# First loads in one ordered queue, with the other queue held, in a fused linear-attention and expert-mixture kernel

## The chip, the cores and the metric

The kernel runs on one core of one Trainium2 chip. A core has a matrix engine (TensorE, "PE" in the profile; "PEld" are its weight loads), a vector engine (VectorE, "DVE"), an activation engine (ScalarE, "ACT"), a general engine (GpSimd, "POOL") and a queue engine (SyncE, "SP") that issues transfers. ACT and POOL can issue transfers too. The metric is the device time of one execution in microseconds; the smaller the better.

## The reference

Inputs are q, k and v, each of 8 batches, 8 heads, 576 rows and 64 columns in float32, and the weights of a mixture of 4 experts (512 to 1024 to 512) with a table of 4608 x 4 expert shares.

```python
phi = lambda x: where(x > 0, x, exp(x) - 1) + 1
kv  = einsum('bhsd,bhse->bhde', phi(k), v);  z = sum(phi(k), axis=2)
x   = einsum('bhsd,bhde->bhse', phi(q), kv) / (einsum('bhsd,bhd->bhs', phi(q), z)[..., None] + 1e-6)
x   = x.transpose(0, 2, 1, 3).reshape(4608, 512)
p   = domain_probs / (domain_probs.sum(-1, keepdims=True) + 1e-9)
out = sum over e of p[:, e:e+1] * (maximum(x @ w1[e], 0) @ w2[e])
```

## The kernel before

**Tiling.** A batch has 512 rows that are handled as a tile of 128 partitions x 4, and 64 remaining rows (the "rest"). Attention runs by pairs of heads, four pairs to a batch: `load_pair` loads k, q and v of one pair (256 KB each), `load_rest` the rest rows of k, v and q of all heads (128 KB each). `attention` maps k and q (an exponential on ACT, L468, and two DVE steps, L452 and L453), multiplies k and v (L511 to L519; the ninth matmul, L519, takes the rest rows, and needs the tile `vpr`), copies the product to `kvz` (ACT, L530 and L531), turns q on PE (L480) and copies it (L493), forms numerator and denominator (L544, L546) and normalises on DVE (L551, L552). Each pair gives 128 columns of x.

**Stages.** Batch 0 comes first and fast. Its x is turned on PE (`turn_x`, L667), copied by ACT (L672) and goes through all four experts with plain matmuls: `first_l1` (L677; 32 products of 512 columns an expert, expert 0 with its first 16 products taken column block by column block, as x arrives) and `first_l2` (L687). Meanwhile batch 1's attention runs between them, and DVE forms sums of weights (L629, L650) for a scheme of seven instead of eight block products. From then on 64 units, each half a batch and one expert, go through `l1_seven` (L831) and `l2_unit` (L907) in that scheme, with the attention of batches 2 to 7 in between; U(n) is the due time of unit n. The last unit ends with a chain of six DVE sums (L973) and four stores of 128 KB.

**What sets the order.** All work is entered in a plan (`Plan.add`) with engine, assumed duration, priority, what it reads and writes, and for a transfer an assumed time `move`. `Plan.order` lays the list out twice in a model of the engines (`lay_out`), the second time with due times worked out backwards, and emits the instructions in the order of the planned start; each engine then runs its own instructions strictly in that order. POOL's are kept in the order in which they were entered. In the model all transfers share one line: `mover` is when it is next free. The plan's times decide the order of instructions and nothing else; on the chip an instruction starts when its semaphores allow.

**First transfers.** Rest k of batch 0 goes out on ACT's queue. Pair 0's k, v and q go out on SP's. On POOL's queue go k of pair 1, the rest of v (converted to 16 bits by the transfer, straight into `vpr`), v and q of pair 1, then pairs 2 and 3, the weights of expert 0, and everything else up to batch 1. Pair 3 and batch 1 reuse buffers of earlier pairs. From batch 2 on loads use SP's queue; those of batch 2 and the rest loads of batches 2 and 3 wait until the last weight block has landed (`hold`, `mark`).

Each POOL transfer also waits for the landing of the one eight places ahead of it, which shows in the waits of POOL for `w`.

## Time and profile before

| | us |
|---|---|
| time, median of 4 runs (lowest to highest) | 499.72 (499.67 to 500.68) |
| the profiled execution: its time | 500.68 |
| the profiled execution: its span | 498.9 |
| PE busy / PEld busy | 480.3 / 425.1 |
| DVE / ACT / POOL busy | 410.6 / 366.9 / 42.3 |
| PE's first matmul | 6.50 |
| first product of the seven-product scheme, unit 0 | 82.4 |
| last PE product starts / last DVE sum starts | 492.9 / 494.4 |

The span reaches from the first to the last instruction of the program; the execution's time has 1.8 us more around it. Times in the traces count from the start of the span. A tile's name stands without its buffer's number: `kq` holds k and q of a pair, `xp`, `u`, `vs` and `kqr` likewise are load buffers, `l1b` and `l2b` are accumulators of the two layers, and parts of `s` serve as the identity and as `kvz` of pairs 2 and 3. In a table by stages the first column is the stretch, then its length, and for each engine the busy time with the count of instructions. In a timeline a row gives start, duration, engine and line, then what is written and read, and in brackets the idle time before it with what ended it. A row can merge several equal instructions.

### The profile page before, as it was taken

Reading aid. Unit: us, or ns where it says so; the run is one execution under the profiler, and the core shown is the slowest. Engines: PE = TensorE matmul, PEld = TensorE weight load, DVE = VectorE, ACT = ScalarE, POOL = GpSimd, SP = SyncE. Lnnn points to the kernel's source line nnn. Section 1 sums busy time; section 2 is a strip of 40 time slices with the busy share of each in tenths; the row PEclk is TensorE's granted clock in tenths of the full one; section 3 lists DMA queues with packets and bytes.
Section 4 is the critical chain, followed back from the end, with each engine's and each line's share of the span. In section 5 each row is a group of like instructions: output and inputs, shape, how many; then the busy total and the mean of one; then the engine's idle time right before and its main releaser. Section 6 shows DMA issues by size and latency. Waiting matters only on the chain.

```text
span 498.9 us, 14890 instructions
## 1 busy us (share of the span) xinstructions
PE 480.3 (96%) x6040; PEld 425.1 (85%) x6040; DVE 410.6 (82%) x1033; ACT 366.9 (74%) x690; POOL 42.3 (8%) x68
## 2 busy tenths in 40 slices
PE   1899999999999999999999999999999999999995
PEld 1544546999999999999999999999999999999995
DVE  6668899999899999889998998899988675767664
ACT  5546668988987698769976988789766767676641
POOL 7666600000000000000000000000000000000000
PEclk9999999999999999999999999999999999999998
DMA  9999959958865586574558565666733333334221
GB/s 232 197 236 225 259 109 214 204 122 168 165 159 138 129 138 139 137 170 120 153 125 183 122 150 129 149 162 121 159 54 76 55 86 34 96 44 77 54 43 43
DMA packets 125574, 67.04 MB, mean 134 GB/s; under 512 B 95521, under 2 KB 119601, under 8 KB 125505
## 3 DMA queue, kind: packets, MB, share of 16 engines
q1 hardware_dynamic: 115056, 51.53, 47.8%
q0 software_dynamic: 9760, 14.17, 14.1%
q8 instruction: 47, 0.77, 0.6%
q10 hardware_dynamic: 688, 0.39, 0.3%
q14 instruction: 23, 0.18, 0.1%
HBM read 45.16 MB, written 9.44 MB: 109 GB/s over the span
## 4 chain that ended last, share of the span: by engine, by line
PE 88%; DMA 4%; ACT 3%; DVE 2%; POOL 1%; issue 1%; DVEq 0%; POOLq 0%; ACTq 0%
PE l1b L831 40%; PE l2b L907 38%; PE l1b L677 4%; PE l2b L687 3%; DMA w<-in_moe_w_dram 2%; PE at L567 1%; DMA vpr<-in_v_dram 1%; PE at L516 1%; ACT xp L791 1%; POOL w L261 1%; DVE ot L973 0%; DVE kqp L453 0%; DVE kqp L452 0%; ACT ek L468 0%; ACT s L672 0%
## 5 line engine op out<-in xcount | busy, mean ns | idle before, releaser
L831 PEld LDWEIGHTS <-w 128*128 128x128 f16 x2048 | 134.2, 98 | 5.4
L907 PE MATMUL l2b<-w,h 128*128 128x256 f16 x768 | 115.0, 273 | 0.0
L907 PE MATMUL l2b<-t,s 128*128 128x256 f16 x768 | 114.7, 273 | 0.0
L845 ACT ACTIVATE h<-l1b 128x512 f16<-128x512 f32 x128 | 76.6, 598 | 51.2 <-PE l1b L831 45.8
L831 PEld LDWEIGHTS <-w1x 128*128 128x128 f16 x1536 | 100.4, 98 | 4.4 <-issue 0.8
L907 PEld LDWEIGHTS <-s 128*128 128x128 f16 x1024 | 90.1, 98 | 6.2
L851 DVE CUSTOM_DVE_ANT_0 h<-l1b,p 128x512 f16<-128x512 f32 x64 | 44.2, 691 | 43.6 <-PE l1b L831 40.7
L831 PE MATMUL l1b<-xs,w1x 128*128 128x128 f16 x1024 | 78.1, 219 | 0.3 <-ACT l1b L848 0.3
L831 PE MATMUL l1b<-xT,w 128*128 128x128 f16 x1024 | 78.0, 219 | 0.0
L831 PE MATMUL l1b<-xs,w 128*128 128x128 f16 x1024 | 78.0, 219 | 0.0
L791 ACT ACTIVATE xp<-x,p_nat 128x512 f16<-128x512 f16 x112 | 77.6, 721 | 0.5
L907 PEld LDWEIGHTS <-h 128*128 128x128 f16 x768 | 67.3, 98 | 4.7 <-ACT h L845 0.2
L893 DVE TENSOR_TENSOR s<-h 128x512 f16<-128x512 f16 x128 | 53.8, 420 | 2.1
L848 ACT COPY l1b<-l1b 128x512 f32<-128x512 f32 x64 | 36.8, 575 | 13.8 <-PE l1b L831 13.4
L848 ACT COPY u<-l1b 128x512 f32<-128x512 f32 x64 | 37.4, 585 | 11.2 <-PE l1b L831 10.9
L851 DVE CUSTOM_DVE_ANT_0 h<-l1b,u 128x512 f16<-128x512 f32 x64 | 43.7, 684 | 1.3 <-PE l1b L831 0.4
L848 ACT COPY p<-l1b 128x512 f32<-128x512 f32 x64 | 37.4, 584 | 8.2 <-PE l1b L831 7.6
L809 DVE TENSOR_TENSOR xs<-xT,xs 128x256 f16<-128x256 f16 x128 | 36.9, 288 | 3.9
L468 ACT ACTIVATE ek<-kq 128x512 f16<-128x512 f32 x60 | 37.7, 630 | 2.7 <-DMA kq<-in_k_dram 1.8
L831 PE MATMUL l1b<-xT,w1x 128*128 128x128 f16 x512 | 39.0, 219 | 0.0
L907 PE MATMUL l2b<-w,s 128*128 128x256 f16 x256 | 38.4, 273 | 0.0
L893 DVE TENSOR_TENSOR s<-s,h 128x512 f16<-128x512 f16 x64 | 27.1, 424 | 6.3 <-ACT h L845 0.5
(127 smaller groups left out, 566.2 us busy)
## 6 DMA issues: line engine op xcount, KB each, us to landing
w<-in_moe_w_dram POOLq DMA_DIRECT2D x32, 256.0 KB, 8.0
out_dram<-ot SPq DMA_DIRECT2D x16, 512.0 KB, 2.7
kq<-in_k_dram SPq DMA_DIRECT2D x25, 256.0 KB, 3.2
vs<-in_v_dram SPq DMA_DIRECT2D x25, 256.0 KB, 3.8
kq<-in_q_dram SPq DMA_DIRECT2D x25, 256.0 KB, 3.2
kq<-in_k_dram POOLq DMA_DIRECT2D x5, 256.0 KB, 7.2
kq<-in_q_dram POOLq DMA_DIRECT2D x5, 256.0 KB, 6.1
xT<-xp SPq DMA_TRANSPOSE x64, 3.1
```

The source lines that it names most:

```text
L261: i = eng.dma_start(out=out_, in_=in_)
L468: pl.add("ACT", 0.55, pri + i * step, lambda i=i: nc.scalar.activation(ek[:, i], kq[:, i], AF.Exp), r=(sk[i],), w=(("ek", ei, i),))
L677: nc.tensor.matmul(out=bank, lhsT=w1_sb[e][:, dc, fj * P : (fj + 1) * P], rhs=xt0[:, dc, :], start=(dc == 0), stop=(dc == DC - 1),)
L687: nc.tensor.matmul(out=bank, lhsT=hts[ht[fj]][:, c * P : (c + 1) * P], rhs=w2_sb[e][:, fj, :], start=(fj == 0), stop=(fj == FC - 1),)
L791: pl.add("ACT", 0.6, pri, lambda c=c, src=src, ps=ps: nc.scalar.activation(xp[:, c, :], src, AF.Copy, scale=ps), r=r, w=(("xp", xi, c),))
L809: lambda o=o, a=a, b_=b_: tt(out=o, in0=a, in1=b_, op=AO.subtract),
L831: nc.tensor.matmul(out=bank[:, fc * P : (fc + 1) * P], lhsT=wt[:, kc, fc * P : (fc + 1) * P], rhs=r[:, kc, :], start=(start and fc == 0 an ...
L845: return lambda: nc.scalar.activation(o, bank, AF.Relu)
L848: return lambda: nc.scalar.copy(o, bank)
L851: return lambda: nc.vector._custom_dve(TENSOR_ADD_SAT, out=o, in0=bank, in1=t, s0=BIG, s1=0.0)
L893: pl.add("DVE", 0.36, U(n + 1) + d - 0.5, lambda i=i, a=a, b_=b_, alu=alu: tt(out=s4[:, i], in0=a, in1=b_, op=alu), r=r, w=(Q(i),))
L907: nc.tensor.matmul(out=l2b[bank][:, half * HD : (half + 1) * HD], lhsT=a[:, c, :], rhs=w[:, c], start=(opens and first and c == 0), stop=( ...
```

## The change

First transfers: pair 0's loads and the rest loads of k and v all go out on SP's queue, in the order k, rest k, q, rest v, v. In batch 0 each pair's q goes ahead of its v on either queue. POOL's first load, k of pair 1, waits until k of pair 0 has landed (mark "k0"); the mark that batch 2 waits for is now named "w". The rest of v of batch 0 arrives in float32 and ACT converts it into `vpr`, as it did for the other batches already.

The plan: `mover` becomes one line for each queue. Where two queues overlap, both are made longer. Assumed transfer times change (rest loads 0.75 to 1.1, w1 1.4 to 1.28, w2 1.55 to 1.3), as does the limit past which a landing is assumed 1.9 later. Priorities of batch 0's attention, of `turn_x` and of expert 0's first layer change.

The end: in the last unit's source order P6 stands ahead of P5, one of two ACT copies goes away, and the second DVE sum reads P5 from its accumulator in place of that copy.

Lines move by up to 6, so that L519 of before is L525 after, and L973 is L977.

```diff
@@ -87,7 +87,7 @@
         ready = {e: {} for e in free}
         fixed = {"POOL": [n for n, o in enumerate(ops) if o["eng"] == "POOL"]}
         at = [o["after"] for o in ops]
-        mover = 0.0
+        mover = dict.fromkeys(free, 0.0)
 
         def release(n):
             ready[ops[n]["eng"]][n] = at[n]
@@ -118,8 +118,13 @@
             start[n] = max(t, at[n])
             free[e] = done = start[n] + o["dur"]
             if o["move"]:
-                mover = max(done + o["lead"], mover) + o["move"]
-                done = mover + self.LAND + (0.0 if mover < 80 else 1.9)
+                begin = max(done + o["lead"], mover[e])
+                other = "POOL" if e != "POOL" else "SP"
+                shared = mover[other] > begin
+                if shared:
+                    mover[other] += o["move"]
+                mover[e] = begin + o["move"] * (1 + shared)
+                done = mover[e] + self.LAND + (0.0 if begin < 70 else 1.9)
             o["start"], o["done"] = start[n], done
             for u in users[n]:
                 lat = self.HOP if ops[u]["eng"] != e or o["move"] else 0.03
@@ -253,18 +258,18 @@
 
     last = {}
 
-    def dma(queue, pri, out_, in_, w, move, r=(), hold=False, mark=False, after=0.0):
+    def dma(queue, pri, out_, in_, w, move, r=(), hold=None, mark=None, after=0.0):
 
         eng = {"POOL": nc.gpsimd, "SP": nc.sync, "ACT": nc.scalar}[queue]
 
         def go():
             i = eng.dma_start(out=out_, in_=in_)
             if mark:
-                last["mark"] = i.ins.name
+                last[mark] = i.ins.name
             if hold:
                 tc.add_manual_dep(
                     i.ins,
-                    last["mark"],
+                    last[hold],
                     mybir.DependencyInfo(
                         mybir.DependencyClass.Sync, mybir.DependencyReason.DATA
                     ),
@@ -276,8 +281,8 @@
             0.72 if queue == "POOL" else 0.5,
             pri,
             go,
-            r=r + (("mark",) if hold else ()),
-            w=w + (("mark",) if mark else ()),
+            r=r + ((("mark", hold),) if hold else ()),
+            w=w + ((("mark", mark),) if mark else ()),
             move=move,
             after=after,
         )
@@ -289,41 +294,42 @@
         flat = vss[i].rearrange("p h c d -> p (h c d)").bitcast(FP16)
         return flat[:, 0 : 2 * C * D].rearrange("p (h c d) -> p h c d", h=2, c=C)
 
-    def load_pair(b, pr, queue, pri, after=0.0, first=None):
+    def load_pair(b, pr, queue, pri, after=0.0, hold=None):
         hs = slice(2 * pr, 2 * pr + 2)
         n = 3 if b < 2 else 2
         i = rot("stage%d" % n, n) if n == 2 else rot("stage3", 3)
         stage[b, pr] = i
         kk = stage_keys(i)
         vo = vss[i] if b or queue == "SP" else v16(i)
-        for t, o, key in ((k, kqs[i][:, 0], kk[0]), (v, vo, kk[2]), (q, kqs[i][:, 1], kk[1])):
+        parts = [(k, kqs[i][:, 0], kk[0]), (v, vo, kk[2]), (q, kqs[i][:, 1], kk[1])]
+        if b == 0:
+            parts[1:] = parts[:0:-1]
+        for t, o, key in parts:
+            if (b, pr, key) == (0, 0, kk[1]):
+                load_rest(0, "SP", 0, parts=(0,))
             keys = (key, "v00") if (b, key) == (1, ("st", 1, 2)) else (key,)
             dma(queue, pri, o, t[b, hs, 0:NT].rearrange("h (p c) d -> p h c d", c=C), keys, 0.7,
-                hold=b == 2, after=after)
-            if first is not None and key == kk[0]:
-                first()
+                hold="w" if b == 2 else hold if key == kk[0] else None,
+                mark="k0" if (b, pr, key) == (0, 0, kk[0]) else None, after=after)
 
     def load_rest(b, queue, pri, after=0.0, parts=(0, 1, 2)):
         par = b % 2
         rs = slice(par * R, par * R + R)
         for i in parts:
             t, o = ((k, kqr[rs, 0]), (v, vr[rs]), (q, kqr[rs, 1]))[i]
-            key = ("str", par, i)
-            if b == 0 and i == 1:
-                o, key = vprs[0][rs, :, 0:D], ("vpr", 0)
-            dma(queue, pri, o, t[b, :, NT:S].rearrange("h s d -> s h d"), (key,), 0.75,
-                hold=b in (2, 3), after=after)
+            dma(queue, pri, o, t[b, :, NT:S].rearrange("h s d -> s h d"), (("str", par, i),), 1.1,
+                hold="w" if b in (2, 3) else None, after=after)
 
     def load_w1(e, dcs):
         for dc in dcs:
             dma("POOL", 0, w1_sb[e][:, dc, :], moe_w1[e, dc * P : (dc + 1) * P, :],
-                (("w1", e, dc, 0), ("w1", e, dc, 1)), 1.4)
+                (("w1", e, dc, 0), ("w1", e, dc, 1)), 1.28)
 
     def load_w2(e):
         src = moe_w2[e].rearrange("(f p) d -> p f d", p=P)
         for c in range(0, FC, 2):
             dma("POOL", 0, w2_sb[e][:, c : c + 2, :], src[:, c : c + 2, :],
-                (("w2", e, c // 2, 0), ("w2", e, c // 2, 1)), 1.55, mark=(e, c) == (3, 6))
+                (("w2", e, c // 2, 0), ("w2", e, c // 2, 1)), 1.3, mark="w" if (e, c) == (3, 6) else None)
 
 
     src_p = moe_domain_probs.rearrange("(b s) e -> s b e", s=S)
@@ -374,7 +380,7 @@
             sk, ek, key = ("str", par, 2 * i), ("ek", ei, i), ("kpr", "qpr")[i]
             pl.add("ACT", 0.55, pri + i * 0.5, lambda i=i: nc.scalar.activation(
                 er[rs, i], kqr[rs, i], AF.Exp), r=(sk,), w=(ek,))
-            if i == 0 and b:
+            if i == 0:
                 pl.add("ACT", 0.55, pri + 0.1, lambda: nc.scalar.copy(
                     vprs[par][rs, :, 0:D], vr[rs]), r=(("str", par, 1),), w=(("vpr", par),))
             pl.add("DVE", 0.92, pri + 0.5 + i * 0.5, lambda i=i: maps(i), r=(sk, ek), w=(key,))
@@ -925,7 +931,7 @@
         if first:
             seq = (P1, P5, P2, P6, P7, P4, P3)
         elif end:
-            seq = (P1, P5, P6, P7, P4, P2, P3)
+            seq = (P1, P6, P5, P7, P4, P2, P3)
         p0 = U(n + 1) + 0.45
         for i, (bank, half, a, ak, w, wk, opens) in enumerate(seq):
             pl.add("PE", 0.436, p0 + 0.9 * i,
@@ -942,10 +948,8 @@
         s1, s5 = (s15[:, i : i + 1].broadcast_to([P, 2, HD]) for i in range(2))
         sk = ("s15", "ident", ("kvz", 2), ("kvz", 3))
         if end:
-            for i in range(2):
-                pl.add("ACT", 0.36, p0 + i, lambda i=i: nc.scalar.copy(
-                    s15[:, i], l2b[0][:, i * HD : (i + 1) * HD]), r=(("p", 0, i),),
-                    w=(("s15", i),) + (() if i else sk))
+            pl.add("ACT", 0.36, p0, lambda: nc.scalar.copy(s15[:, 0], l2b[0][:, 0:HD]),
+                   r=(("p", 0, 0),), w=sk)
         else:
             pl.add("ACT", 0.5, p0 + 3.5, lambda: nc.scalar.copy(
                 s15.rearrange("p a d -> p (a d)"), l2b[0]), r=("l2b0",), w=sk)
@@ -959,8 +963,8 @@
         if end:
             lo, hi = (lambda bank: l2b[bank][:, 0:HD]), (lambda bank: l2b[bank][:, HD : 2 * HD])
             for dur, o, a_, b_, r, w in (
-                (0.4, of[:, 0], hi(1), s15[:, 0], (("p", 1, 1), ("s15", 0)), (O(0),)),
-                (0.3, of[:, 1], of[:, 0], s15[:, 1], (("s15", 1),), (O(0),)),
+                (0.4, of[:, 0], hi(1), s15[:, 0], (("p", 1, 1), "s15"), (O(0),)),
+                (0.4, of[:, 1], hi(0), of[:, 0], (("p", 0, 1),), (O(0),)),
                 (0.62, of[:, 2:4], lo(3)[:, None].broadcast_to([P, 2, HD]), of[:, 0:2],
                  (("p", 3, 0), O(0)), (O(2),)),
                 (0.4, of[:, 2], hi(2), of[:, 2], (("p", 2, 1),), (O(2),)),
@@ -1007,9 +1011,9 @@
     for i in range(2):
         pl.add("DVE", 0.27, 26 + 10 * i, lambda i=i: nc.vector.memset(qTr[i], 0.0),
                w=[("qTr", i, pr) for pr in range(DC)])
-    load_rest(0, "ACT", 0, parts=(0,))
     load_pair(0, 0, "SP", 0)
-    load_pair(0, 1, "POOL", 0, first=lambda: load_rest(0, "POOL", 0, parts=(1,)))
+    load_rest(0, "SP", 0, parts=(1,))
+    load_pair(0, 1, "POOL", 0, hold="k0")
     load_pair(0, 2, "POOL", 0)
     rest_maps(0, True, 3, (0,))
     for pr in range(DC):
@@ -1019,13 +1023,13 @@
             probs(0, 2, p5_b, ("p5",), "pnat0", 24)
             load_w2(0)
             load_rest(0, "POOL", 0, parts=(2,))
-        attention(0, pr, True, 2.5 + 4 * pr, 0.4, two=True)
-        turn_x(pr, 6 + 4 * pr)
+        attention(0, pr, True, 2.5 + pr, 0.4, two=True)
+        turn_x(pr, 4.9 + pr)
     rest_maps(0, True, 28, (1,))
     rest_late(30)
     load_w1(1, range(DC))
     load_w2(1)
-    ht = first_l1(0, 15, 0.2, 4)
+    ht = first_l1(0, 17.5, 0.1, 4)
     first_l2(0, ht, 22, 0.9, True)
     sums_w1(0, U(0) - 6)
     sums_w2(0, U(1) - 6)
```

## The prediction

> **What bounds the kernel now.** I read the page's chain of work first. It is TensorE for nearly the whole span:
>
> ```profile
> PE 88%; DMA 4%; ACT 3%; DVE 2%; POOL 1%; issue 1%; DVEq 0%; POOLq 0%; ACTq 0%
> ```
>
> So only time in which TensorE (PE) has no work can be won. The table by stages (stretch, its length, busy time of PE, PEld, DVE, ACT, POOL with counts, granted clock, DMA share, GB/s) tells where that is:
>
> ```profile
> 0.00:6.50 6.50, 0.00 (x1) 0.01 (x1) 4.30 (x18) 2.94 (x4) 5.49 (x13) 1.00 0.78 194
> 6.50:9.19 2.69, 0.69 (x8) 0.63 (x9) 0.98 (x3) 1.15 (x2) 1.77 (x3) 1.00 1.26 252
> 9.19:12.57 3.38, 1.50 (x15) 1.07 (x14) 2.27 (x6) 2.85 (x9) 2.62 (x5) 1.00 1.13 293
> 12.57:16.15 3.58, 3.33 (x37) 3.00 (x38) 2.57 (x8) 3.26 (x8) 3.58 (x6) 1.00 1.04 177
> 16.15:20.22 4.07, 3.19 (x29) 1.95 (x29) 2.01 (x5) 1.49 (x5) 2.04 (x4) 1.00 1.14 188
> 20.22:24.94 4.72, 3.93 (x28) 1.94 (x28) 3.29 (x9) 2.26 (x5) 2.01 (x5) 1.00 1.23 217
> 24.94:82.38 57.44, 56.83 (x309) 27.36 (x309) 48.10 (x108) 36.17 (x70) 24.80 (x37) 1.00 0.96 199
> 82.38:492.00 409.62, 409.33 (x5605) 388.03 (x5604) 344.67 (x874) 316.79 (x593) 0.00 (x0) 1.00 0.56 121
> ```
>
> After 24.94 us PE idles 0.6 + 0.3 us in 467. Before that it idles 6.5 us, then 18.44 - 12.64 = 5.8 us more. The chain in order of time (start, length, what) says what the 5.8 us hang on, and the timeline shows the waits:
>
> ```profile
> 2.56 6.59 DMA vpr<-in_v_dram
> 11.93 0.59 ACT qT L493
> 15.52 0.59 ACT s L672
> 19.59 0.59 ACT s L672
> 23.25 0.59 ACT s L672
> 24.94 3.61 PE l1b L677 x16
> ```
>
> ```profile
> 1.30 0.83 POOL L261 DMA_DIRECT2D kq<-in_k_dram  x1 [0.36 <-issue]
> 9.19 0.27 PE L519 MATMUL l2b<-vpr,kqpr 128*128 128x130 f16 x1 [2.00 <-DMA vpr<-in_v_dram]
> 19.13 0.21 ACT L530 CAST s<-l2b 64x65 f16<-64x65 f32 x1 [2.54 <-PE l2b L546]
> 20.22 0.59 PE L677 MATMUL l1b<-s,w 128*128 128x512 f16 x2 [0.89 <-ACT s L672]
> ```
>
> PE meets its first matmuls at 6.50 and stops at the ninth until the 64 remaining rows of v (vpr), sent on POOL's queue at 2.56, land at 9.15. From there one chain of short steps across PE, ACT and DVE reaches 24.94: pair 0's numerator at 12.57, its x turned at 14.29, its copy at 15.52, first expert's products at 16.15, and, since PE's queue is in order, pair 3 behind them (x of pair 3 copied at 23.25, last products 23.88). The weights do not set it: expert 0's w1 blocks land at 14.97 to 19.42.
>
> **What the Trainium skill says.** "DMA: Bandwidth & Descriptors", section "Issuing engines are not separate DMA queues": loads of all queues run on the same 16 DMA engines and interleave. The trace agrees: with three queues loading, q of pair 0 needs 6.9 us from issue to landing, against 3.0 to 3.1 us for the same load at 90 us. So an order by waits can speed the first tiles, but makes no bandwidth. "TensorE: Matmul & The Clock Gate", Part 1: the array runs at half rate until a window of about 3.4 us has been busy. The trace agrees in kind: 512-column matmuls start 0.43 us apart at 16 us and 0.216 us from 20 us on; the change falls at 18.3, 5.7 us after PE's unbroken work began at 12.57. (The clock column shows 1.00 throughout and does not tell it.)
>
> **The change, part by part.**
>
> *SP's five loads (k, rest of k, q, rest of v, v), POOL held until k lands.* SP's issues last 0.46 us for a 256 KB load and 0.64 to 0.76 us for a rest load, so they stand at 0.74, 1.26, 2.0, 2.6 and 3.3. With landings from rows of this trace (k 3.0; rest 3.5 to 3.7; q and v 3.0 to 3.8): k at 3.7, rest of k 4.8, q 5.1 to 5.5, rest of v 6.2, v 6.6. Before: 3.71, 4.48, 8.65, 9.15, 5.07. ACT loses the 0.72 us issue of the rest of k, which lay before its first data: nothing.
>
> *ACT's extra cast* (vpr, once a DMA that converted): 64x512 takes 0.60 us on ACT at 124.4. ACT's order is now exp k, exp rest k, exp q, cast vpr, cast v: with 0.63 us each from 4.8 on, 3.7-4.3, 4.8-5.5, 5.5-6.1, 6.2-6.8, 6.8-7.4. That is on the path: pair 0's k-v product (its nine matmuls 0.6 us) starts at 7.4 and ends at 8.1; before it ended at 9.46. q is turned ahead of it, at 6.9.
>
> *Pair 0.* exp k of pair 1 stands first (7.7-8.4), then the copies of qT (0.59) and kvz (0.44): the numerator at 9.4, before 12.57: 3.1 us earlier. Normalising waits for DVE's q map of pair 1 (to 10.5); x turned 11.5 (before 14.29), copied 12.95 (before 15.52).
>
> *POOL's stream, held.* Its first load goes out at 3.7, not 1.30, and in front of it nothing else is lost: the constants and the identity are built ahead. Behind it stand all loads of pairs 1 to 3 and all weights; ACT, DVE and PE wait for these. The quickest POOL load here took 3.9 us (9.95 to 13.81), the first one 6.6 against the other queues' traffic. SP's loads are over by 6.6, so I take 4.0: k of pair 1 at 7.7 (before 7.88), each further load 0.70 us on, pair 3's last at 13.3 (before 13.81, with vpr's small rows in between), first w1 at 14.5 (14.97). With 6.6 us instead these are 10.3 and 17.1: that end costs 1.6 us of the gain below and goes into the range. Below 3.9 us I see no reason for a gain.
>
> *Pairs 1 to 3.* In the changed program pair 1's turning and x come before expert 0's first product, and that product is spread between pairs 2 and 3. Walking PE, ACT and DVE in their new order with this trace's durations (exp 0.65 from start to start, map 0.95, normalise 0.93, copies 0.5 to 0.6, numerator 0.56 at half rate and 0.33 at full, 0.43 or 0.216 per product) and full rate from 18.4: pair 3's k-v product 15.8 (before 17.81), its numerator 18.9 (21.31), its x copied 21.0 (23.25), expert 0's last four products 21.6 (23.88), the run of 16 at 22.6 (24.94). The same walk over the old order with the old landings gives 24.8, so it is 0.15 short; I compare walk with walk: **24.8 - 22.6, some 2.2 us**.
>
> *What hides the rest, 25 to 82 us.* PE is now 2.2 us early; the loads must be too. Slack of before: w1 of expert 1, last block, landed 30.7, used 33.9: 3.2. k of batch 1's pair 1: 46.8 and 49.3: 2.4. Its v: 47.5 and 49.8: 2.3. Last w1 of experts 2 and 3: 4.5 and 4.9. DMA engines are full in this stretch (share 0.96), so the stream moves only by its head, 0 to 0.5 us early. The smallest slack, 2.3, just covers 2.2. DVE is the other cover: 14.06 of 15.20 us busy at 58.8 to 74, PE waits 0.59 for it at 67.5; but that stretch starts with DVE itself waiting for PE (58.8), so it moves along. I charge 0.2 us. The longer plan times for rest loads and the shorter ones for weights issue nothing; they reorder DVE and ACT most at 75 to 125, where DVE runs at 0.9: PE's stall of before there is 0.3; I take it unchanged, -0.2 to +1.0.
>
> *Tail.* PE's seven last products stand in the same order in both programs (P1, P5, P6, P7, P4, P2, P3): the swap in the source does not come through. One ACT copy of 0.33 us goes:
>
> ```profile
> 491.33 0.65 ACT L946 COPY s<-l2b 128x256 f32<-128x256 f32 x2 [0.71 <-PE l2b L907]
> 491.82 0.42 DVE L973 TENSOR_TENSOR ot<-l2b,s 128x256 f32<-128x256 f32 x1 [0.33 <-ACT s L946]
> 492.35 0.42 DVE L973 TENSOR_TENSOR ot<-ot,s 128x256 f32<-128x256 f32 x1
> ```
>
> DVE's first sum needs only the first copy and P6; the second starts 0.11 us after it: 0 to 0.1 us won. I take 0.
>
> **Sum.** -2.2 + 0.2 = -2.0 us. The profiled execution took 500.68 us, 498.9 of it span and 1.8 around it: span 496.9, execution 498.7. The median of the four runs is 0.96 us under the profiled one: 499.72 - 2.0 = **497.7 us**. About 0.2% (1.0 us) is what a measurement of this kernel can tell from no change.
>
> **Rivals.**
>
> *Late full rate (small gain).* PE has holes of 0.4 us until 14.3 in the new walk, as it had before 12.57. If the 5.7 us count from there, full rate comes at 20 to 21: each cold product costs 0.215 us; the run of 16 starts at 23.8, gain 1.0, 498.7. For it: the trace's dense 5.7 us. Against: the array is three quarters busy from 9.4, so it can as well come at 16, which gives 21.5: gain 3.3, 496.4.
>
> *Swallowed later (no change).* POOL's first load takes 6.6 us, or DVE and the loads at 46 to 82 hold PE to the old times: the slack of 2.3 less a head 2.4 us late. 499.2 to 500.2. For it: DMA full, DVE at 0.9. Against: the slacks named.
>
> *Slower: the half rate lasts into the run of 16.* Place: 22 to 28 us; price 0.216 us per 512-column product. It decides from 24 us on, where second-layer work starts at 28.1 as before; full rate at 26 gives 29.4, 1.2 us late: 500.9; at 28, 501.7. For it: a window that is not in step with the program. Against: PE's work has no hole over 0.4 us after 11.5, so the rate would need 12 us.
>
> *The change not doing what it says* holds for the tail alone, as shown.
>
> **How the numbers follow.** Forecast 0.66, its own range 496.6 to 498.7; late rate 0.12; swallowed 0.14; slower 0.08. The range goes down to the early full rate with the tail's 0.1 (496.2) and up over the late rate into the swallowed case: 499.8. Faster by over 0.2% (under 498.7): nearly all of the forecast and half of the late rate, 0.71; same 0.20; slower 0.09.
>
> **What would show it.** Right: k of pair 0 lands near 3.7 and POOL's first issue follows; vpr cast at 6.2-6.8; no 2 us wait at the ninth matmul; numerator of pair 0 near 9.4; run of 16 near 22.6; U(0)'s first product near 80.4 instead of 82.38; PE idle under 1.2 us after it. Wrong: k of pair 1 past 9, full rate after 21, a PE wait of over 1 us for weights, x or DVE at 30 to 125.

## The result, and the profile after

The changed kernel takes 500.62 us (median of 31 runs, 499.55 to 502.31), the kernel before 499.75 (51 runs beside it, 498.56 to 502.81): ratio 1.0018, 95% interval 1.0011 to 1.0025. It is about 0.9 us slower; the forecast was 2.0 us faster. The profiled execution took 500.56, its span is 498.8.

The page's chain of work of the changed kernel, by engine:

```profile
PE 83%; ACT 6%; DVE 6%; DMA 2%; issue 2%; SPq 0%; DVEq 0%; ACTq 0%
```

TensorE still sets the time, but ACT and DVE have 12% of the chain instead of 5%. The table by stages, in the same stretches and columns as before:

```profile
6.50:9.19 2.69, 0.61 (x4) 0.45 (x5) 1.18 (x3) 1.73 (x4) 2.69 (x4) 1.00 1.12 311
9.19:12.57 3.38, 2.56 (x30) 2.20 (x29) 1.73 (x5) 2.84 (x9) 3.38 (x7) 1.00 1.02 287
12.57:16.15 3.58, 2.39 (x25) 1.86 (x25) 2.61 (x7) 3.34 (x9) 3.19 (x5) 1.00 1.11 172
16.15:20.22 4.07, 3.84 (x29) 2.50 (x30) 2.57 (x7) 2.02 (x5) 1.93 (x3) 1.00 1.14 207
20.22:24.94 4.72, 4.22 (x31) 2.27 (x30) 2.71 (x8) 2.13 (x5) 2.37 (x5) 1.00 1.24 218
24.94:82.38 57.44, 57.37 (x324) 28.13 (x323) 49.41 (x111) 36.04 (x71) 24.86 (x37) 1.00 0.99 206
82.38:492.00 409.62, 408.47 (x5589) 387.33 (x5589) 342.98 (x873) 315.91 (x592) 0.00 (x0) 1.00 0.55 121
```

From 6.5 to 24.94 TensorE is busy for 13.62 us instead of 12.64, and yet only 0.23 us come out of it (below): much of the busy time is at half rate. From 82.38 on it idles 1.15 us instead of 0.29. The timeline, with the waits:

```profile
4.05 0.84 POOL L266 DMA_DIRECT2D kq<-in_k_dram  x1 [2.74 <-DMA kq<-in_k_dram]
8.61 0.62 ACT L468 CAST vs<-vs 128x512 f16<-128x512 f32 x1 [0.89 <-DMA vs<-in_v_dram]
9.28 0.27 PE L517 MATMUL l2b<-vs,kqp 128*128 128x128 f16 x1 [1.13 <-ACT vs L468]
10.62 0.27 PE L550 MATMUL at<-kvz,qT 128*128 128x128 f16 x1 [0.53 <-ACT kvz L537]
16.36 0.61 PE L673 MATMUL l2b<-s,x 128*128 128x128 f16 x4 [0.60 <-DVE x L558]
16.99 0.61 PE L683 MATMUL l1b<-s,w 128*128 128x512 f16 x1
20.70 0.43 PE L683 MATMUL l1b<-s,w 128*128 128x512 f16 x1
24.71 1.46 PE L683 MATMUL l1b<-s,w 128*128 128x512 f16 x6
231.43 0.61 PE L837 MATMUL l1b<-xs,w1x 128*128 128x128 f16 x8 [0.34 <-ACT l1b L854]
```

The 2 us stop at the ninth matmul is gone, and pair 0's numerator comes at 10.62 instead of 12.57. But v of pair 0, last of SP's five loads, lands at 8.59 and holds the k-v product to 9.28; POOL's first load goes out at 4.05, and the first w1 block lands at 16.94 instead of 14.97. Expert 0's first product is at 16.99 (16.15 before), its products stand 0.43 us apart until 20.7 (18.3 before), and the run of 16 starts at 24.71 (24.94).

What the first product hangs on is told by the chain of work in order of time (start, length, what):

```profile
3.37 5.22 DMA vs<-in_v_dram
10.62 0.27 PE at L550
15.62 0.70 DVE x L558
16.36 0.61 PE l2b L673 x4
```

It is v of pair 0 and the steps of pairs 0 and 1 behind it. The first w1 block landed 0.05 us before TensorE came to it, and no wait for it shows.

The tail:

```profile
491.30 0.37 ACT L951 COPY s<-l2b 128x256 f32<-128x256 f32 x1 [0.71 <-PE l2b L913]
491.79 0.42 DVE L977 TENSOR_TENSOR ot<-l2b,s 128x256 f32<-128x256 f32 x1 [0.33 <-ACT s L951]
494.24 0.41 DVE L977 TENSOR_TENSOR ot<-l2b,ot 128x256 f32<-128x256 f32 x1
```

The last sum starts at 494.24 instead of 494.35, with TensorE's end 0.03 earlier: under 0.1 us won.

By these two profiles the kernels are equal (500.56 and 500.68), while the medians differ by 0.9 us. So the profile of before is not a typical one, and the experiments begin there.

### The profile page after: what moved, and what is told of

Same layout as the page of the kernel before. It is cut to its first block, busy times and chain, and to the rows that moved or that the text cites. A ratio compares the mean times of both kernels' runs of the same rounds, so it can differ in the third digit from the quotient of the medians.

```text
span 498.8 us, 14868 instructions
## 1 busy us (share of the span) xinstructions
PE 480.9 (96%) x6040; PEld 425.8 (85%) x6040; DVE 409.9 (82%) x1033; ACT 366.6 (74%) x690; POOL 41.6 (8%) x67
## 4 chain that ended last, share of the span: by engine, by line
PE 83%; ACT 6%; DVE 6%; DMA 2%; issue 2%; SPq 0%; DVEq 0%; ACTq 0%
PE l1b L837 34%; PE l2b L913 33%; PE l1b L683 6%; PE l2b L693 5%; ACT xp L797 2%; PE at L573 1%; DVE h L857 1%; PE at L522 1%; DMA vs<-in_v_dram 1%; DVE s L899 1%; ACT h L851 1%; DMA xT<-xp 1%; ACT ek L381 1%; DVE xs L815 1%; ACT ek L474 1%
## 5 line engine op out<-in xcount | busy, mean ns | idle before, releaser
L857 DVE CUSTOM_DVE_ANT_0 h<-l1b,p 128x512 f16<-128x512 f32 x64 | 44.1, 689 | 42.9 <-PE l1b L837 40.5
L913 PEld LDWEIGHTS <-h 128*128 128x128 f16 x768 | 67.5, 98 | 4.5
L459 DVE TENSOR_TENSOR kqp<-ek,kqp 128x512 f16<-128x512 f16 x64 | 27.2, 425 | 7.0 <-ACT ek L474 2.7
```

Source lines behind the costliest of these rows:

```text
L459: nc.vector.tensor_tensor(out=o, in0=ek[:, i], in1=o, op=AO.min)
L857: return lambda: nc.vector._custom_dve(TENSOR_ADD_SAT, out=o, in0=bank, in1=t, s0=BIG, s1=0.0)
L913: nc.tensor.matmul(out=l2b[bank][:, half * HD : (half + 1) * HD], lhsT=a[:, c, :], rhs=w[:, c], start=(opens and first and c == 0), stop=( ...
```

## The experiments

All ratios are to the kernel before, run beside. In the experiments' kernels line numbers differ by some 5 to 30; operations and tiles are the same. Two marks are used throughout: the start of the run of 16 (end of the early part), and the copies of `u` by ACT, one a unit, which show how far each of the 64 units is ahead or behind.

| kernel | run of 16 | `u` of unit 0 | `u` of unit 63 | time profiled | median (runs) | ratio |
|---|---|---|---|---|---|---|
| before, first profile | 24.94 | 84.50 | 486.48 | 500.68 | 499.75 (51) | |
| before, second profile | 23.71 | 83.27 | 485.23 | 499.53 | | |
| changed, first profile | 24.71 | 83.38 | 486.45 | 500.56 | 500.62 (31) | 1.0018 (1.0011 to 1.0025) |
| changed, second profile | 24.26 | 82.95 | 486.06 | 500.07 | | |
| changed, late order of before | 24.53 | 83.21 | 485.30 | 499.36 | 499.85 (14) | 1.0006 (0.9995 to 1.0016) |
| loads alone | 25.83 | 85.39 | 487.41 | 501.80 | 501.66 (5) | 1.0048 (1.0036 to 1.0060) |
| before, hold alone | 26.41 | 85.97 | 487.93 | 502.18 | 502.38 (6) | 1.0058 (1.0043 to 1.0073) |
| before, late order of changed | 23.89 | 84.60 | 488.29 | 502.84 | 502.84 (5) | 1.0063 (1.0050 to 1.0076) |
| changed, late order of before, no hold | 27.94 | 86.80 | 488.91 | 503.00 | 502.85 (6) | 1.0061 (1.0044 to 1.0077) |
| changed, late order of before, v ahead of q | 24.42 | 83.03 | 485.86 | 499.94 | 500.53 (22) | 1.0018 (1.0009 to 1.0026) |
| changed, late order of before, first warming | 25.50 | 84.24 | 487.09 | 501.25 | 500.18 (22) | 1.0011 (1.0002 to 1.0021) |
| changed, late order of before, warmed | 23.32 | 82.66 | 485.48 | 499.62 | 500.41 (13) | 1.0018 (1.0007 to 1.0028) |
| before, warmed | 23.32 | 82.88 | 484.94 | 499.23 | 499.16 (21) | 0.9987 (0.9980 to 0.9995) |
| before, warmed, middle order of changed | 23.32 | 82.04 | 484.01 | 498.29 | 498.17 (12) | 0.9974 (0.9965 to 0.9982) |

The marks come from one execution each. Where its time is off the median by half a microsecond or more, they are not those of a typical one: the first warming was profiled 1.1 us above its median, the warmed changed kernel 0.8 below.

**The kernel before, a second profile.** The kernel unchanged.

> The kernel before once more, unchanged, for a second profile: its first profiled execution took 500.68, near 1 us over its median. If the early part varies from run to run, this profile shows another start of unit 0 than 82.4 (81.4 for a run at the median), with the change of spacing to full rate or the landing of the rest of v at another time; if the variation lies later, unit 0 starts at 82.4 again and the units drift apart after it.

Its execution took 499.53, at the median. The timeline:

```profile
8.57 0.27 PE L519 MATMUL l2b<-vpr,kqpr 128*128 128x130 f16 x1 [0.89 <-DMA vpr<-in_v_dram]
15.68 1.05 PE L677 MATMUL l1b<-s,w 128*128 128x512 f16 x3 [0.25 <-ACT s L672]
16.57 0.38 PE L677 MATMUL l2b<-s,w 128*128 128x512 f16 x1
23.71 3.61 PE L677 MATMUL l1b<-s,w 128*128 128x512 f16 x16
```

The rest of v landed 0.6 us earlier than in the first profile, the full rate came by 16.4 instead of 18.3 (within the first three products, of which the last two start at 16.06 and 16.35), and the run of 16 is 1.23 us earlier. Every unit after it is 1.23 to 1.27 us earlier, from the first to the last. So the variation lies in the first 24 us, and the profile on which the forecast was built was 1.2 us late there. A third execution with the same early part, that of the mirror below, has 23.89. The typical run of 16 of the kernel before is at 23.7 to 23.9, not 24.9; 23.7 is used from here on.

**The changed kernel, a second profile.** Unchanged as well.

> The changed kernel once more, for a second profile. The two profiles of the kernel before differ by 1.2 us in the first 24 us (the change of spacing to full rate at 18.3 and at 16.6, the rest of v landed at 9.15 and at 8.5) and by nothing after that. The first profile of the changed kernel is at its median (500.56 against 500.62), so I expect the run of 16 at 24.3 to 25.0 again, and the stalls in the units at the same places (near 127, 231 and 320 to 345), since these are in the order and not in the run.

It took 500.07; run of 16 at 24.26, full rate at 20.3. The waits of 0.21 at 82.1, 0.43 at 127.3 and 0.34 at 231.0 are there again. Between 316 and 345 TensorE was busy for 29.00 of 29.00 us in either profile: what I had read as stalls there was only an ACT copy at another place in its unit. Against the second profile of before, the changed kernel's early part is 0.55 to 1.0 us *later*.

**Late order of before.** What the plan starts after 75 us stands in the order of the kernel before; all else is as changed.

```diff
@@ Plan.order
-        return self.lay_out()
+        new = self.lay_out()
+        late = [self.ops[i] for i in self.late()]
+        ids = {id(o) for o in late}
+        todo = [o for o in new if id(o) not in ids] + late
...
+        return todo
```

> The changed kernel, but what its plan starts after 75 us is put in the order in which the plan of the kernel before has it (loads, holds and the first 75 us as changed). Theory A (the new plan's order costs what the early part won): the stalls of 0.34 us at 231 and of 0.2 us at 82.5 and those between 320 and 345 us go, every unit from 8 on starts 0.6 to 0.8 us ahead of the kernel before, to the end: ratio to before 0.9985, against 1.0018 for the changed kernel. Theory B (the late order is worth nothing, run-to-run changes of the early part set the median): ratio 1.0015 to 1.002 again.

1.0006, where the changed kernel has 1.0018: some 0.6 us by the ratios, whose intervals overlap. The profiles are clearer: from `u` of unit 0 to that of unit 63 the changed kernel takes 403.07 and 403.11 us, with the late order of before 402.09, which is 1.0 us less. The number expected, 0.9985, was wrong, because it counted from the late profile of before. The groups of the products that wait show the difference; in the changed kernel:

```profile
L837 PE MATMUL l1b<-xs,w1x 128*128 128x128 f16 x1024 | 78.0, 219 | 1.1 <-ACT l1b L854 1.0
```

and with the late order of before:

```profile
L853 PE MATMUL l1b<-xs,w1x 128*128 128x128 f16 x1024 | 78.0, 219 | 0.3 <-ACT l1b L870 0.3
```

The idle time before one group of products is 1.1 against 0.3 us, all of it waiting for ACT's copy of the first accumulator. At 231, ACT first takes an exponential of a rest load (228.92), a copy to `xp` (229.57) and a relu (230.20), and then that copy (230.81). The plan's changed times issue nothing, but place such steps elsewhere. Which of the changed times does it was not separated.

**The mirror.** The kernel before, with what follows 75 us in the order of the changed kernel's plan (the same edit, with the other list).

> The mirror of the first run: the kernel before, with its own loads and its own first 75 us, but what follows 75 us in the order in which the changed kernel's plan has it. Theory A (that order costs 0.6 to 1.1 us by itself, through ACT and DVE steps that stand ahead of those TensorE waits for): ratio 1.0012 to 1.002, with a stall of 0.3 us or more near 231 and between 320 and 345. Theory B (the order costs only together with the changed kernel's early start): 0.9995 to 1.0005.

1.0063, some 3.1 us: more than expected. Its early part is that of a typical run (23.89), so all of it comes later: 1.15 us before `u` of unit 0, 1.7 in the units. The same group of products waits 2.2 us, half of it for DVE's differences of x (`xs`), at one place. The timeline there, on DVE and TensorE:

```profile
80.75 0.43 DVE L468 TENSOR_SCALAR kqp<-kq 128x512 f16<-128x512 f32 x1 [1.95 <-DMA kq<-in_q_dram]
83.07 1.14 PE L847 MATMUL l1b<-xs,w1x 128*128 128x128 f16 x14 [1.14 <-DVE xs L825]
```

DVE stands idle for q of batch 2, which goes out at 76.85, in the place that the kernel before gives it on SP's queue; in the changed kernel it goes out at 69.56. So this part comes from joining the two orders at 75 us. It says that an order costs more under arrivals for which it was not laid out, and not that the late order by itself costs 3.1.

**Loads alone.** The loads of the changed kernel (one queue, hold, q ahead of v, the rest of v cast by ACT) and its tail, with the order that the old model, times and priorities give for the first 26 us and the order of before after it. The whole order is handed to the plan as a list.

```diff
@@ Plan.order
-        return self.lay_out()
...
+        todo = [self.ops[i] for i in self.given()]
...
+        return todo
@@ Plan.lay_out
-                begin = max(done + o["lead"], mover[e])
...
-                done = mover[e] + self.LAND + (0.0 if begin < 70 else 1.9)
+                mover = max(done + o["lead"], mover) + o["move"]
+                done = mover + self.LAND + (0.0 if mover < 80 else 1.9)
@@
-        attention(0, pr, True, 2.5 + pr, 0.4, two=True)
-        turn_x(pr, 4.9 + pr)
+        attention(0, pr, True, 2.5 + 4 * pr, 0.4, two=True)
+        turn_x(pr, 6 + 4 * pr)
...
-    ht = first_l1(0, 17.5, 0.1, 4)
+    ht = first_l1(0, 15, 0.2, 4)
```

> The loads of the changed kernel (one queue, hold, q ahead of v, the rest of v cast by ACT) and its tail, with the plan's model, times and priorities of before for the first 26 us and exactly the order of before after it. Theory A (the loads themselves cost in the early part): run of 16 at 24.5 to 25.0, against 23.7 for a run of the kernel before near its median; u of unit 0 copied 59.5 later; ratio 1.0015 to 1.002, all of the change's loss without any of its plan. Theory B (the new early order spoils what the loads win): run of 16 at or ahead of 23.7, ratio 0.999 to 1.000.

1.0048, more than the whole change loses. Its timeline:

```profile
17.31 0.61 PE L692 MATMUL l1b<-s,w 128*128 128x512 f16 x1 [0.22 <-DMA w<-in_moe_w_dram]
25.83 3.40 PE L692 MATMUL l1b<-s,w 128*128 128x512 f16 x15
68.40 0.40 PE L495 MATMUL l2b<-s,kqp 128*128 128x128 f16 x4 [0.59 <-DVE kqp L468]
```

The first w1 block lands at 17.27 and expert 0's first product waits for it; the run of 16 is 2.1 us behind a typical run of before, and stays 2.1 to 2.2 behind to the end, with the wait of 0.59 for DVE that the kernel before has at 66 to 67.5 and the changed one lacks. So theory A holds, and more: under the old order the loads cost 2.1 us, and the new order up to 75 us wins some 2.1 of it back, 1.3 before the run of 16 (25.83 against 24.53) and 0.9 between it and unit 0.

**The hold alone.** The kernel before, every instruction in its order, with POOL's first load held until k of pair 0 has landed.

```diff
-                hold=b == 2, after=after)
+                hold=b == 2 or (b, pr, key) == (0, 1, kk[0]),
+                mark=(b, pr, key) == (0, 0, kk[0]), after=after)
```

> The kernel before, every instruction in its order, with POOL's first load held until k of pair 0 has landed, and nothing else. Theory A (the hold makes POOL's stream late and that is what the early part waits for): k of pair 1 lands at 8.2 to 8.6 (7.4 to 7.9 without), the rest of v at 9.2 to 9.6 (8.5 to 9.15), the first w1 block at 16.0 to 17.0 (14.7 to 15.0), q of pair 0 at 5.5 to 6.5 in place of 8.3 to 8.65; run of 16 0.5 to 1.0 later, at 24.3 to 24.9; ratio 1.001 to 1.002. Theory B (the early q makes up for it): run of 16 within 0.3 of 23.7, ratio 0.9995 to 1.0005.

1.0058, worse than expected. Its timeline:

```profile
13.23 0.29 PE L559 MATMUL at<-kvz,qT 128*128 128x128 f16 x1 [2.41 <-ACT qT L508]
26.41 0.81 PE L692 MATMUL l1b<-s,w 128*128 128x512 f16 x3
```

q of pair 0 lands at 6.07 (8.29 in the second profile of before), as hoped; but v of pair 1 lands at 9.45 (8.91), its q at 10.20 (9.66), k of pair 2 at 11.85 (10.41), and the first w1 block at 16.84 (14.66). POOL's first load goes out 2.9 us later (4.19 for 1.30), but k of pair 1 lands only 0.25 later (7.61 for 7.36): the lateness grows along the queue, to 2.2 at the weights. TensorE meets the late pairs, not the early q: 2.7 us lost. Against the 2.1 of all the loads, the other changes to the loads would together win some 0.6; they were not separated further, and the early orders of the two runs differ.

**No hold.** The changed kernel with the late order of before, every instruction in its order, without the hold.

```diff
-    load_pair(0, 1, "POOL", 0, hold="k0")
+    load_pair(0, 1, "POOL", 0)
```

> As the run with the late order of before, with every instruction in the same order, but POOL's first load no longer waits for k of pair 0. Theory A (the hold makes POOL's whole stream late): POOL's first load goes out near 1.3 in place of 4.05, k of pair 1 lands near 7.9, pair 3's loads end near 13.6 (14.57 when held), the first w1 block at 15 to 15.5 (16.94), first product of expert 0 near 15.5 to 16 (16.99), and the run of 16 near 24.0 (24.71): 0.5 to 0.7 us faster than with the hold. Theory B (SP's five loads suffer what POOL's win): v of pair 0 lands at 9.5 to 10.5 in place of 8.6, pair 0's numerator at 11.5 to 12.5, and the run of 16 does not move.

Theory A fell; theory B named the right mechanism, and missed its size by far. The timeline, on TensorE and POOL:

```profile
12.86 0.27 PE L533 MATMUL l2b<-vs,kqp 128*128 128x128 f16 x1 [3.12 <-ACT vs L484]
13.11 0.72 POOL L282 DMA_DIRECT2D vs<-in_v_dram  x1 [3.40 <-ACT vs L484]
27.94 2.32 PE L699 MATMUL l1b<-s,w 128*128 128x512 f16 x10
```

v of pair 0 lands at 12.17, behind POOL's loads; its cast holds TensorE for 3.1 us and POOL's queue for 3.4, since pair 3's v reuses that buffer. The first w1 block lands at 18.31. So with five loads in line on SP, and an order laid out for the hold, the hold is needed, and is worth 3.4 us at the run of 16; without the five in line it costs 2.7. Queue and hold belong together, and together they cost 2.1 under the old order.

**v ahead of q.** With the late order of before, SP's source order is k, rest k, v, rest v, q; in the plan's order rest v goes out just ahead of v.

```diff
-            parts[1:] = parts[:0:-1]
+            parts[1:] = parts[1:] if pr == 0 else parts[:0:-1]
         for t, o, key in parts:
-            if (b, pr, key) == (0, 0, kk[1]):
+            if (b, pr, key) == (0, 0, kk[2]):
                 load_rest(0, "SP", 0, parts=(0,))
+            if (b, pr, key) == (0, 0, kk[1]):
+                load_rest(0, "SP", 0, parts=(1,))
...
-    load_rest(0, "SP", 0, parts=(1,))
```

> As the run with the late order of before, but on SP's queue v of pair 0 goes ahead of rest v and q (k, rest k, v, rest v, q). Theory A (v, last of five and sharing with POOL's first loads, is what is late): v lands at 6.4 in place of 8.6, its cast is done before 7.2, pair 0's k-v product starts at 7.6 (9.28 in the changed kernel), its numerator waits for q (landing 8.6, mapped 9.9, turned, copied) and comes at 11 to 11.5: 0.4 to 0.9 later than the 10.62 of the changed kernel. Theory B (any of the five that stands last is as late, only the sum counts): the same, so first product of expert 0 unchanged at 17.0, because the w1 block sets it, and ratio within 0.0005 of the run with the late order alone.

```profile
7.51 0.27 PE L535 MATMUL l2b<-vs,kqp 128*128 128x128 f16 x1 [7.51 <-ACT vs L486]
16.57 0.63 PE L701 MATMUL l1b<-s,w 128*128 128x512 f16 x1
24.42 2.75 PE L701 MATMUL l1b<-s,w 128*128 128x512 f16 x12
```

Rest v landed at 6.26, v at 6.82, and the k-v product came 2 us earlier than in the kernel with the late order alone (9.50). Expert 0's first product is only 0.4 us earlier, since it could not start ahead of 16.41, where the first w1 block lands; the numerator of pair 0, which now waits for q, is at 11.01 (10.84), and the run of 16 is 0.1 earlier: theory B there. In the ratio B missed: 1.0018 (1.0009 to 1.0026) is 0.0012 above the run with the late order alone, not within 0.0005. From `u` of unit 0 to that of unit 63 it takes 402.83 us for 402.09. Most of this comes at two places, 171.5 and 301.6, where products wait for DVE to normalise x (0.18 and 0.17 us) and fall 0.34 us behind each time. By tiles and shapes, TensorE, ACT and DVE have their work in the same order in both kernels there; why DVE is late is open.

**Warming TensorE.** Idle products of 512 columns into an accumulator that is not in use yet; their results are overwritten. First 12 ahead of the first work and six in the gaps of the first three pairs, then 20 and 28 (the edit shown, of which the calls in the gaps are left out), to leave hardly a gap. Both tries have the late order of before.

```diff
+    FILL = dict(start=(20,), turn=(5, 2, 4, 0), mid=(0, 0, 0, 0), kv=(4, 2, 0, 0), num=(0, 0, 0, 0), tx=(4, 7, 0, 0))
+
+    def fill(key, pr=0):
+        for _ in range(FILL[key][pr]):
+            nc.tensor.matmul(out=l1b[2], lhsT=xT_b[2][:, 0, 0],
+                             rhs=xT_b[2][:, 0].rearrange("p c t -> p (c t)"), start=True, stop=True)
...
+    nc.vector.memset(xT_b[2][:, 0], 0.0)
+    fill("start")
```

> As the run with the late order of before, with 12 idle products of 512 columns on TensorE ahead of its first work (into an accumulator that is not in use yet; their results are overwritten) and seven more in the gaps of the first two pairs' work. Theory A (the half rate to 20.7 us is a warm-up that begins when the array becomes busy): the change of spacing from 0.43 to 0.22 us falls among the idle products, before 8 us, pair 0's numerator takes 0.33 us, the products of expert 0 stand 0.22 us apart from the first at 17.0, and the run of 16 starts near 23.0 to 23.5 (24.71): ratio 0.996. Theory B (the full rate comes at a fixed time or is set by something else): it still comes at 18 to 21 us and the ratio stays at that of the run with the late order alone.

The first try warmed the array and lost it again. Timeline, and table by stages of the same run:

```profile
17.23 0.61 PE L707 MATMUL l1b<-s,w 128*128 128x512 f16 x1 [1.39 <-DMA w<-in_moe_w_dram]
```

```profile
13.00:15.00 2.00, 1.33 (x22) 1.00 (x22) 1.45 (x5) 1.99 (x6) 2.00 (x4) 1.00 1.19 153
15.00:17.00 2.00, 0.53 (x4) 0.26 (x4) 1.78 (x5) 1.36 (x3) 0.74 (x1) 0.61 0.99 177
17.00:19.00 2.00, 1.77 (x19) 1.45 (x20) 0.00 (x0) 0.00 (x0) 0.99 (x2) 0.50 1.13 210
```

Idle products are 0.43 us apart until 5.0 and 0.21 from 5.3 on, after 4.1 us of unbroken work. In the thin work from 12 to 15.4 the rate is lost; the clock column shows it (0.61, 0.50), and it comes back at 22.2. The run of 16 starts at 25.50. The wait of 1.39 for w1 is new: a TensorE that is not slowed comes to the block before it lands. Ratio 1.0011 (1.0002 to 1.0021). The profiled execution, at 501.25, lies 1.1 us above the median (runs from 498.55 to 501.81), so the rate need not be lost every time.

> As the warmed run before, with idle products in every gap of TensorE's work up to expert 0's first product (20 ahead of the first work, then 5, 4, 2, 2, 4, 4 and 7 in the gaps, 0.22 us each at full rate). In the first warmed run the full rate came at 5.3 us, was lost again at 15.4 in the gap before the first w1 block landed, and came back only at 21.9. Theory A (the rate is kept if no gap is left, and the half rate behind the late first product is what the early part of the changed kernel loses): granted clock 1.00 from 10 to 30 us, expert 0's products 0.22 apart from the first at 16.5 to 17.2, pair 3's numerator at 19.0 to 19.5 (20.96 in the changed kernel), run of 16 at 22.0 to 22.8: 1.8 to 2.5 us ahead of the same kernel without warming, ratio to before 0.996 to 0.998. Theory B (the first w1 block and pair 3's chain set the end whatever the rate): run of 16 at 24 or later, ratio 1.000 to 1.001. Part of A may be lost to the weights: w2's last block of expert 0 lands at 26.0, expert 1's last w1 block at 31.3.

```profile
16.93 0.38 PE L713 MATMUL l1b<-s,w 128*128 128x512 f16 x1
23.32 3.61 PE L713 MATMUL l1b<-s,w 128*128 128x512 f16 x16
```

The full rate now holds, and the run of 16 starts at 23.32 instead of 24.53: the half rate costs the changed kernel 1.2 us there, by these two executions. It was less than expected (22.0 to 22.8): the first product still waits for its w1 block (16.81), and behind it TensorE waits 0.23 us for DVE's x at 19.1 and 0.46 for ACT's copy of it at 22.3. And the 1.2 us do not last: `u` of unit 0 is 0.55 ahead, that of the last unit 0.2 behind the same kernel unwarmed; ratio 1.0018 (1.0007 to 1.0028). Laid beside the unwarmed run, TensorE falls behind by 0.40 us at 40.7 and 0.18 at 44.1, where it meets ACT's relus, and by 0.34 each at 171.2 and 301.2, the two places of the run with v ahead of q.

**The kernel before, warmed.** The same for the kernel before, in its order.

> The kernel before, with every instruction in its order, and idle products on TensorE in its gaps up to expert 0's first product (15 ahead of the first work, 8 ahead of the ninth matmul that waits for the rest of v, then 2, 6, 3 and 1). If the half rate costs both kernels, the products of expert 0 stand 0.22 apart from the first at 15.0 to 15.5 (16.15 at half rate before), and the run of 16 starts near 23.5 to 24.0 (24.94): ratio 0.998. If the half rate is hidden behind pair 3's chain of DVE and ACT steps and its late loads in the kernel before, ratio 0.9995 to 1.0005.

0.9987: 0.4 us ahead of a typical run at the run of 16 (23.32 against 23.71) and 0.3 to the end, 0.65 by the ratio. Between the two theories: the half rate costs the kernel before less at the run of 16, 0.4 against 1.2 us; its full rate comes earlier (16.4 against 20.6). Warmed, the two kernels reach the run of 16 at the same time, 23.32. So where the rate is full, the changed kernel's early part shows no loss. That rests on one execution of each, and that of the changed kernel was a fast one.

**Before, warmed, with the middle order.** To this, what the changed kernel's plan puts between 24 and 75 us in its order (a list in place of the plan's, as in the loads alone).

> The kernel before with its own first 24 us and the idle products of the warmed kernel before, then the order of the changed kernel's plan up to 75 us, then the order of before. Theory A (from the run of 16 to unit 0 the new order is worth 0.6 to 0.9 us: u of unit 0 is copied 58.7 us after the run of 16 starts in the changed kernel, 59.6 in the kernel before, whose turning of q waits 0.59 us for DVE at 66): 58.7 to 59.0 here, no wait at 66, unit 0's copy near 82.1 (82.88 in the warmed kernel before), ratio 0.997. Theory B (the difference comes with the later start of the changed kernel, in which DVE has caught up): 59.5 again and ratio 0.9985 to 0.999, as for the warmed kernel before.

0.9974, the fastest of all: 498.17 us (median of 12 runs) against 499.45. The tables by stages from 24 to 82 us, for the warmed kernel before and with the new order in the middle:

```profile
24.00:82.00 58.00, 57.39 (x327) 28.22 (x326) 48.44 (x110) 36.08 (x71) 24.29 (x36) 1.00 0.95 201
```

```profile
24.00:82.00 58.00, 58.00 (x341) 28.97 (x340) 49.40 (x112) 36.81 (x73) 24.72 (x36) 1.00 0.95 207
```

TensorE no longer waits 0.59 for DVE at 66, and `u` of unit 0 follows the run of 16 by 58.72 instead of 59.56 us, as in the changed kernel (58.67). The 0.9 us stay to the last unit. Theory A; this part of the change is a gain.

## Why the prediction was wrong

The account that the runs give, against a typical run of before: the loads, queue and hold together, +2.1 us (loads alone, under the old order); the new order ahead of the run of 16, -1.1 to -1.6 (25.83 to 24.71 and 24.26); the new order between 24 and 75 us, -0.9; the new order after 75 us, +1.0 by the profiles (0.6 by the ratios); the tail, under -0.1. That is +0.5 to +1.1; the ratio says +0.9. The terms come from single profiles whose early parts vary by some 0.5 us, and the split between loads and order holds for this sequence of exchanges. By the forecast's own steps:

- **"The median of the four runs is 0.96 us under the profiled one: 499.72 - 2.0."** This failed by itself. The 2.0 were measured from a profile whose early part was 1.2 us late (24.94; typically 23.71), and then taken from a median that does not have that lateness. Even with the walk right, 22.6 is 1.1 us from 23.71: some 498.6. The page showed a time 0.2% over the median of the other three runs, and that had to be asked about first. Its POOL loads were late as well: k of pair 1 landed at 7.88, in the four other profiles with these loads at 6.25 to 7.36. Beside 7.88, 7.7 behind a hold looked free.
- **The walk: pair 3's k-v product 15.8, its numerator 18.9, its x copied 21.0, the run of 16 at 22.6.** The first profile of the changed kernel has 17.97, 20.96, 23.01 and 24.71. Numerator 0 is already 1.2 us late (10.62 for 9.4), pair 3's k-v product 2.2, and nothing is added after it. So the walk failed ahead of 18 us, in the landings, and these are the next two terms.
- **"SP's five loads."** k at 3.75 was right (3.7), rest k 5.06 (4.8); q came at 6.38 (5.1 to 5.5), rest v 7.08 (6.2), v 8.59 (6.6). The cast of `vpr` at 7.11 waited for q and rest v (6.2 to 6.8), and numerator 0 came at 10.62 (9.4). On this v the chain up to expert 0's first product hangs. The Trainium skill's sentence that I had cited, "DMA: Bandwidth & Descriptors", section "Issuing engines are not separate DMA queues", holds here too: POOL's loads, released at 4, interleave with SP's last ones, and v took 5.2 us. I had taken 3.0 to 3.8 for q and v. But putting v earlier won only 0.1 us at the run of 16: expert 0's first product then came at 16.57, right behind its w1 block (16.41).
- **"POOL's stream, held."** I took 4.0 us for its first load and the first w1 block at 14.5. The first load took 4.31, k of pair 1 landed at 8.35 instead of 7.7, pair 3's last at 14.57 instead of 13.3, and then 2.4 us passed to the first w1 block at 16.94, the landing that is furthest off. It landed at 16.4 to 17.3 in all eight profiles with a hold, and at 14.1 to 15.0 in all five of the kernel before without one. The other end of my bound, 17.1, met the number by luck: it supposed a first load of 6.6 us. The hold alone costs 2.7 us in the order of before.
- **"Full rate from 18.4."** It came at 20.7 and 20.3, as in the rival of the late rate. The number was wrong, but it is not what made the walk late: the forecast too has the full rate come just ahead of pair 3's numerator (18.4 and 18.9; 20.7 and 20.96). A full rate from the start, which the forecast did not count on, is worth 1.2 us at the run of 16, and nothing at the end.
- **"What hides the rest, 25 to 82 us: I charge 0.2."** Wrong in sign: the new order wins 0.9 here, 0.59 of it the wait for DVE's map that is gone. I had seen the wait of 0.59 at 67.5 and taken it as given.
- **"The longer plan times issue nothing; I take it unchanged, -0.2 to +1.0."** The bound was right, the value taken was not: ACT's copies made TensorE wait 1.1 instead of 0.3 us, and putting the old order back won 1.0 us by the profiles, 0.6 by the ratios. With it back the change is near no difference (1.0006), without it measurably slower (1.0018).
- **Tail: 0 to 0.1.** Right.

None of the forecast's own signs of being wrong came up: k of pair 1 landed at 8.35 (not past 9), the full rate came at 20.7 (not after 21), and TensorE's longest wait from 30 to 125 us is 0.21 (not over 1). Several misses, each below its sign, added up. The rival "swallowed later" came nearest in the number, by a first POOL load of 6.6 us that did not occur. The forecast gave slower 0.09, by a half rate that lasts into the run of 16; the causes that did occur, late landings ahead of 18 us and the plan's order in the steady part, stood only in ranges.

## What to carry to other kernels

Ask first whether the profile shown is a typical execution: if its time is off the median by as much as the effect looked for, find the stage that varies before subtracting from it. A hold in front of a queue can look harmless at the first load behind it (here 0.25 us late) and be costly further on (2.2 us at the weights), so trace the last load on that queue that the early work needs, not the first. When a plan's assumed times change, the order of the steady part changes with them: compare the two orders there, and keep the parts that win; here the middle of the new order, with the old loads and a warmed TensorE, gave 0.9974.

## What was not expected of the hardware

- The onset of the full rate moved by some 2 us between two executions of one kernel (18.3 and 16.4 at the latest). The Trainium skill, "TensorE: Matmul & The Clock Gate", Part 1, says that the window runs freely and that the transition varies from run to run; it gives 0.5 us either way. The swing here is larger, but part of it may follow the rest of v, which landed 0.6 us apart.
- The rate was lost although from 7.7 us on no gap ahead of it was over 0.81 us: from 11 to 15 us TensorE was busy for 2.44 of 4.00 us, and fell to half rate at 15.4, for 6.8 us. In the first 30 us the clock column showed 0.50 only here, where the full rate had been granted once. The half rate at the start of every other run stands in it as 1.00: there the trace's record of the granted clock begins only with the full rate (18.3 and 16.2 in the two profiles of before, 20.8 and 20.1 in those of the changed kernel).
- In the held kernels 1.25 to 2.6 us passed between pair 3's last load and the first w1 block, in the kernel before without a hold 1.14 to 1.16. Later blocks mostly came every 1.25 to 1.3 us. What fills the longer steps is open.
